# State-space scan with a gated feed-forward on one Trainium2 core: the loads and the first matmuls of the head are put in another order, and a token tile is transposed by one DMA

## The chip, the core and the metric

The kernel runs on one core of one Trainium2 chip. The metric is device time in microseconds (us), from launch to end, on that core. A core has five engines, each with its own instruction list that it works off in order: PE (TensorE, matmuls), DVE (VectorE), ACT (ScalarE), POOL (GpSimd) and SP (SyncE, which here only issues DMAs). ACT can issue DMAs too, from the same list as its arithmetic. Matmuls write PSUM banks; DVE and ACT read these out ("evacuate" them) into SBUF.

## The reference

Token count 2048, width D = 448, hidden width F = 1792, all inputs and the output bf16.

```python
x  = A_x
xn = layernorm(x)                               # over the 448 columns
# A: a diagonal complex scan over the 2048 tokens
Lam_bar = exp(exp(log_dt) * Lam)
Bu      = xn @ B_bar.T                          # B_bar = ((Lam_bar - 1) / Lam) * B
h[t]    = Lam_bar * h[t-1] + Bu[t]
s       = 2 * real(h @ C.T) + xn * Dskip
# B: a gated feed-forward
f = (sigmoid(xn @ w_gate) * (xn @ w_up)) @ w_down
out = x + s * silu(f)
```

## The kernel before

**Tiling.** The tokens are 16 tiles of 128 (x tile t is `x_all[:, t, :]`), in four chunks of 512 tokens. For matmuls a chunk must stand transposed, with the 448 columns on partitions: `xnT[c % 3]`, seven slots of 128 partitions by 512 tokens. A slot holds two neighbouring blocks of 64 columns, one on partitions 0 to 63, one on 64 to 127. Slot s holds the blocks s and s + 1, so that every block stands once on the lower and once on the upper half. The weights `wG` (gate) and `wU` (up) hold the first 896 output columns on the lower 64 partitions and the other 896 on the upper 64. One step of the feed-forward (`gu_mm`, lines 699 to 712) makes 2 times 128 output columns: 14 matmuls with 64 rows each, in pairs, one of a pair on each half of the array, into a pair of PSUM banks (`gu[a]`, three pairs; two more single banks are `acc[0]` and `acc[1]`). There are seven gate steps g.0 to g.6 and seven up steps u.0 to u.6 a chunk. A gate step is read out by a Tanh on ACT (line 721), an up step by a multiply on DVE (line 724).

**Order.** The kernel adds each operation with an engine, an estimated cost, what it reads and what it writes to a `Plan`. The planner gives every operation a due time, and builds each engine's list by a simulated run with estimated DMA rates (`rate=`). Two orders are fixed by hand: PE works in the order in which operations are added, and while `pl.seq` is set (the head) DVE does too. DMAs of one queue keep their order as well.

**The head (lines 383 to 412 and 962 to 990).** Eleven matmuls on zeros warm PE. SP and ACT issue the loads: x tile 0 on SP, tile 1 and then tiles 2 and 3 in one DMA on ACT; `wG` in three blocks a half (steps 0 and 1, 2 and 3, 4 to 6), the lower half on SP, the upper on ACT; then everything else on SP: `wU`, x tiles 4 to 7, `wU`, and `dbc` (Dskip copied to all partitions). POOL loads three small vectors.
For each of the tiles 0 to 3: `stats(t)` on DVE (line 424 and 425), `chain(t, 1)` (a square root on ACT, line 450, a copy on POOL, a reciprocal on DVE, line 452), `norm(t)` on DVE (line 469), eight PE transposes into an `acc` bank (`pe_transpose`, lines 501 to 503), and a copy of the bank into `xnT[0]`: on ACT for tile 0 (line 506), on DVE for tiles 1 to 3 (line 509).
`columns` (lines 535 to 563) turns the three small vectors with five tiny matmuls (lines 540 and 542) into per-partition columns, from which POOL makes the scan's coefficients.

PE's list in the head before:

```
warm, T0, T1, columns, g.0 g.1 of tile 0, g.0 g.1 of tile 1, T2, T3,
g.2 of tiles 0 and 1, g.0 g.1 g.2 of tiles 2 and 3, g.3 of all four, g.4 ...
```

(T2 stands for the eight transposes of tile 2.) DVE's list: stats 0 and 1, norm 0 and 1, stats 2 and 3, the copy of T1, the readout of `columns`, norm 2 and 3, the copies of T2 and T3; then `pl.seq` ends.

**Later tiles.** Tiles 4 to 15 are normalised on ACT (line 474) into one of eight buffers `xn`, 512 wide; POOL copies the first 64 columns behind the 448 (line 477), so that the last slot finds block 0 beside block 6; two DMA transposes on SP (`dma_transpose`, lines 510 to 518) fill the even and the odd slots. `skip_row` (line 482, DVE) multiplies `xn` by `dbc`.

Of the kernel before, what the change touches and what calls it, by code (L numbers as in the profile page):

```python
# [18 lines left out]
D = 448  # L19
# [226 lines left out]
def kernel(  # L246
# [39 lines left out]
    NXN = 8  # L286
    xn = [sbt(f"xn{i}", [512]) for i in range(NXN)]
    xnT_raw = [sbt(f"xnT{i}", [7 * L]) for i in range(3)]
    xnT = [flat(t[:], 7, L) for t in xnT_raw]
    hF_raw = [sbt(f"hF{i}", [FT * L]) for i in range(2)]  # L290
# [69 lines left out]
    BLK = {"g": [(0, 2), (2, 4), (4, 7)], "u": [(0, 3), (3, 7)]}  # L360
# [25 lines left out]
    load_w("SP", "g", 0, 0, rate=90e3)  # L386
    load_w("SP", "g", 0, 1)
    load_x(1, 1, "ACT")
    load_x(2, 2, "ACT")
    load_w("ACT", "g", 1, 0, rate=90e3)  # L390
    load_w("SP", "g", 0, 2)
    load_w("ACT", "g", 1, 1)
    load_w("ACT", "g", 1, 2)
# [13 lines left out]
    for h in range(2):  # L407
        load_w("SP", "u", h, 0, rate=215e3)
    load_x(4, 4, rate=140e3)
    for h in range(2):  # L410
        load_w("SP", "u", h, 1, rate=260e3)
    load("SP", "dbc", P * D * 2, dbc[:], A_Dskip.unsqueeze(0).to_broadcast((P, D)))
# [9 lines left out]
    def stats(t):  # L422
        b = t % 3
        add("DVE", 0.6, lambda: V.bn_stats(out=bst[b][:], in_=x_all[:, t, :]), r=[("x", t)], w=[("bst", b)])  # L424
        add("DVE", 0.16, lambda: V.bn_aggr(out=mv[:, t, :], in_=bst[b][:]), r=[("bst", b)], w=[("mv", t)])
# [40 lines left out]
    def norm(t):  # L466
        b = t % NXN
        if t < TPC:
            add("DVE", 0.42, lambda: V.tensor_scalar(out=xn[b][:, 0:448], in0=x_all[:, t, :],
                                                     scalar1=meanf[:, t, :], scalar2=rsd[:, t, :],  # L470
                                                     op0=ALU.subtract, op1=ALU.mult),
                r=[("x", t), ("mf", t), ("rs", t)], w=[("xn", b)])
        else:
            add("ACT", 0.65, lambda: A.activation(xn[b][:, 0:448], x_all[:, t, :], ACT.Identity,
                                                 bias=nmr[:, t, :], scale=rsd[:, t, :]),
                r=[("x", t), ("rs", t), ("nm", t)], w=[("xn", b)])
            add("POOL", 0.2, lambda: G.tensor_copy(out=xn[b][:, 448:512], in_=xn[b][:, 0:64]),
                r=[("xn", b)], w=[("xnw", b)])
# [5 lines left out]

    acc_n = [0]
# [9 lines left out]
    def pe_transpose(t):  # L495
        b, a, js = t % NXN, next_acc(), slice(t * P, t * P + P)
        tp = flat(acc[a][:].bitcast(BF16)[:, 0:7 * P], 7, P)

        def f():
            for s in range(6):  # L500
                T.transpose(tp[:, s, :], xn[b][:, s * H:s * H + P], ident[:, :])  # L501
            T.transpose(tp[0:H, 6, :], xn[b][:, 384:448], ident[:, :])
            T.transpose(tp[H:P, 6, :], xn[b][:, 0:H], ident[:, :])
        add("PE", 0.46, f, r=[("xn", b), "ident"], w=[("acc", a)])
        if t == 0:
# [6 lines left out]
    def dma_transpose(t):  # L512
# [4 lines left out]
        tload([k + ("a",)], xnT[c % 3][:, 0:7:2, js], xn[b][:], P * 1024, r=[("xn", b), ("xnw", b)] + al)  # L517
        tload([k + ("b",)], xnT[c % 3][:, 1:6:2, js], xn[b][:, 64:448], P * 768, r=[("xn", b)] + al)
# [16 lines left out]
    def columns(a):  # L535
        vps = flat(gu[a][:, 0, 0:12], 4, 3)
# [6 lines left out]
        add("PE", 0.4, f, r=["ident"] + [("vrow", k) for k in range(3)], w=[("gu", a)])  # L543
        pv = sbt("pv", [3, 4], FP32)
        dt_b = C("dt", 4, BF16)
        add("DVE", 0.1, lambda: V.tensor_copy(out=pv[:].rearrange("p k i -> p i k"), in_=vps[:]), r=[("gu", a)], w=["pv"])
# [20 lines left out]
    def silu_table():  # L567
        add("ACT", 1.3, lambda: A.preload_act_table_set("silu_and_others"), r=[("sd", t) for t in range(4)], w=["silutab"])
# [128 lines left out]
    SW = 0.1  # L697

    def gu_mm(c, k, m, a, lo, hi, first):
        x = xnT[c % 3]  # L700
        ts = slice(lo * P, hi * P)
# [3 lines left out]
        def f():  # L705
            for s in range(7):
                T.matmul(gu[a][:, 0, ts], lhsT=w_[0:H, s, ms], rhs=x[0:H, s, ts], start=(s == 0), stop=(s == 6))  # L707
                T.matmul(gu[a][:, 1, ts], lhsT=w_[H:P, (s + 1) % 7, ms], rhs=x[H:P, s, ts],  # L708
# [3 lines left out]
                   r=xr(c, lo, hi) + [("w", k, 0, m), ("w", k, 1, m)], w=[("gu", a)], name=f"{k}{c}.{m}")  # L712
# [3 lines left out]
    def gu_evac(c, k, m, a):  # L716
# [3 lines left out]
        if k == "g":  # L720
            add("ACT", act(1024), lambda: A.activation(th, gu[a][:], ACT.Tanh, scale=0.5),  # L721
                r=[("gu", a)], w=[tk])
        else:
            add("DVE", dve1(1024), lambda: V.scalar_tensor_tensor(out=ho, in0=th, scalar=1.0, in1=gu[a][:],  # L724
                                                                 op0=ALU.add, op1=ALU.mult),
                r=[("gu", a), tk], w=[hk])
# [23 lines left out]
    def b_phase(c, mid=None):  # L750
# [5 lines left out]
        rs = [(slice(0, H), 6), (slice(H, P), 5)]  # L756
# [14 lines left out]
        def fulls(pt, first):  # L771
            for i in range(2):
                for kt in range(3):
                    if pt < 3:
                        T.matmul(gu[slots[pt]][:, i, :], lhsT=bT[:, kt, i, pt * P:pt * P + P], rhs=x[:, 2 * kt, :],  # L775
                                 start=(first and kt == 0), stop=(not first and kt == 2))
                    else:
                        T.matmul(acc[a3[i]][:, 0:256], lhsT=bT6[:, kt, :],  # L778
                                 rhs=x[:, 2 * kt, i * 256:i * 256 + 256], start=False, stop=(kt == 2))
# [184 lines left out]
    pl.seq = True  # L964
    stats(0)
    stats(1)
    for t in (0, 1):
        chain(t, 1)
        norm(t)
    stats(2)  # L970
    stats(3)
# [3 lines left out]
    columns(slots0[2])  # L975
    for t in (2, 3):
        chain(t, 1)
        norm(t)
    for j in range(2):
        for m in range(2):  # L980
            gu_mm(0, "g", m, slots0[m], j, j + 1, not (j or m))
    pe_transpose(2)
    pe_transpose(3)
    silu_table()
    pl.seq = False
    gu_mm(0, "g", 2, slots0[2], 0, 2, True)
    for m in range(3):
        gu_mm(0, "g", m, slots0[m], 2, 4, False)
        gu_evac(0, "g", m, slots0[m])
    b_load()  # L990
    def stats_for(c):
        for t in range(4 * c, 4 * c + 4):
            if c not in (3,):
                stats(t)
# [16 lines left out]
    for i in range(3, 13):  # L1011
# [83 lines left out]
```

## Time and profile before

| what | us |
|---|---|
| median of three runs | 185.86 (185.44, 185.86, 187.11) |
| span of the profiled execution | 183.7 |
| PE busy | 177.4 |
| DVE busy | 166.4 |
| ACT busy | 94.8 |
| POOL busy | 34.2 |

The span runs from the first to the last instruction of one profiled execution; the median of the runs is 2.2 us longer, for what lies around it. Times below are from the start of that span. The granted TensorE clock was 1.000 over the span.

### The profile page before, as it was taken

What the parts mean: (1) busy time and instruction counts of PE and PEld (TensorE: products, weight loads), DVE (VectorE), ACT (ScalarE), POOL (GpSimd) and SP (SyncE); (2) the same over time, 40 slices, a digit from 0 to 9 for tenths busy, and PEclk for the clock granted to TensorE, in tenths of its full rate; (3) what the DMA queues carried; (4) which work ended last, traced back from release to release, by engine and by line L of the source; (5) the groups of instructions that cost most, each with busy time, mean ns of one, the idle gap of its engine ahead of it and who ended that gap; (6) DMA issues with size and microseconds to landing.
All of it is one profiled execution on the core that took longest, in us unless ns stands there. A gap on an engine that the chain in (4) does not pass through costs nothing.

```text
span 183.7 us, 3601 instructions
## 1 busy us (share of the span) xinstructions
PE 177.4 (97%) x1402; PEld 90.4 (49%) x1402; DVE 166.4 (91%) x296; ACT 94.8 (52%) x152; POOL 34.2 (19%) x95
## 2 busy tenths in 40 slices
PE   7699999999999999999999999999999999999992
PEld 2585555465554444455554444444555444455551
DVE  3873899899999998999999999999999998999973
ACT  3689993958599978665310452367120445211100
POOL 7370465000048557700000000000000000000000
PEclk9999999999999999999999999999999999999999
DMA  5999994489801370243000000002000000001121
GB/s 137 255 225 223 155 166 90 90 256 266 231 0 26 74 82 21 50 82 71 0 2 0 29 0 0 4 0 75 0 4 0 25 25 5 25 0 52 57 73 50
DMA packets 30258, 13.44 MB, mean 73 GB/s; under 512 B 19744, under 2 KB 30240, under 8 KB 30240
## 3 DMA queue, kind: packets, MB, share of 16 engines
q1 hardware_dynamic: 28336, 12.05, 30.7%
q10 hardware_dynamic: 1808, 1.15, 2.5%
q8 instruction: 11, 0.18, 0.4%
q14 instruction: 7, 0.06, 0.1%
q0 software_dynamic: 96, 0.00, 0.0%
HBM read 6.77 MB, written 1.84 MB: 47 GB/s over the span
## 4 chain that ended last, share of the span: by engine, by line
PE 93%; DMA 3%; DVE 1%; issue 1%; POOL 1%; DVEq 0%; POOLq 0%
PE gu L707 45%; PE gu L903 14%; PE acc L932 11%; PE acc L903 9%; PE gu L775 8%; DMA hF<-in_A_Lambda_re_dram 3%; PE gu L708 2%; PE acc L778 2%; PE gu L761 2%; POOL hF L353 1%; PE acc L501 0%; DVE o_t L948 0%; PE acc L764 0%; DVE o_t L944 0%; DVE o_t L941 0%
## 5 line engine op out<-in xcount | busy, mean ns | idle before, releaser
L708 PE MATMUL gu<-xnT,wG 64*128 64x512 bf16 (+2 forms) x245 | 46.0, 333 | 0.0
L707 PE MATMUL gu<-xnT,wG 64*128 64x512 bf16 (+2 forms) x245 | 46.0, 333 | 0.0
L707 PE MATMUL gu<-xnT,wU 64*128 64x512 bf16 x196 | 45.8, 376 | 0.0
L708 PE MATMUL gu<-xnT,wU 64*128 64x512 bf16 x196 | 45.8, 376 | 0.0
L721 ACT ACTIVATE sig<-gu 128x1024 f32<-128x1024 f32 x21 | 21.3, 1021 | 22.0 <-PE gu L708 21.9
L903 PEld LDWEIGHTS <-hF 128*128 128x128 bf16 x224 | 21.9, 98 | 20.7 <-issue 0.2
L707 PEld LDWEIGHTS <-wG 64*128 64x128 bf16 x245 | 21.9, 94 | 18.7
L707 PEld LDWEIGHTS <-wU 64*128 64x128 bf16 x196 | 18.4, 94 | 22.1
L724 DVE SCALAR_TENSOR_TENSOR hF<-sig,gu 128x1024 bf16<-128x1024 f32 x21 | 25.5, 1216 | 2.9 <-PE gu L708 1.6
L903 PE MATMUL gu<-wd,hF 128*128 128x448 bf16 x140 | 27.9, 352 | 0.0
L842 DVE TENSOR_TENSOR_SCAN wv<-c_r,st,z 128x512 bf16<-128x512 f32 x18 | 22.9, 1276 | 0.0
L932 PE MATMUL acc<-cT,hT 128*128 128x448 bf16 (+1 forms) x112 | 22.6, 346 | 0.0
L708 PEld LDWEIGHTS <-wG 64*128 64x128 bf16 x245 | 21.8, 94 | 0.0
L909 ACT ACTIVATE g_t<-gu 128x448 bf16<-128x448 f32 x10 | 5.4, 541 | 29.2 <-DVE o_t L946 12.9
L708 PEld LDWEIGHTS <-wU 64*128 64x128 bf16 x196 | 18.4, 94 | 0.0
L789 ACT CAST bus<-gu 128x1024 bf16<-128x1024 f32 x12 | 11.9, 1011 | 12.4 <-PE gu L761 12.2
L903 PE MATMUL acc<-wd,hF 128*128 128x448 bf16 x84 | 16.9, 352 | 0.0
L775 PE MATMUL gu<-xnT,bT 128*128 128x512 bf16 x72 | 16.7, 379 | 0.0
L932 PEld LDWEIGHTS <-hT 128*128 128x128 bf16 x119 | 11.5, 98 | 10.1 <-issue 0.4
L424 DVE BATCH_NORM_STATS2 bst<-x_all 128x6 f32<-128x448 bf16 x12 | 7.0, 610 | 5.7 <-DMA x_all<-in_A_x_dram 5.7
L795 ACT CAST bus<-acc 64x256 bf16<-64x256 f32 (+1 forms) x24 | 8.8, 369 | 6.4 <-PE acc L778 6.1
L944 DVE TENSOR_TENSOR o_t<-acc,xd 128x448 bf16<-128x448 f32 (+1 forms) x16 | 9.6, 601 | 1.3 <-PE acc L932 1.2
(138 smaller groups left out, 240.1 us busy)
## 6 DMA issues: line engine op xcount, KB each, us to landing
out_dram<-o_t SPq DMA_DIRECT2D x15, 112.0 KB, 1.7
wd<-in_B_w_down_dram SPq DMA_DIRECT2D x2, 784.0 KB, 5.5
x_all<-in_A_x_dram SPq DMA_DIRECT2D x3, 448.0 KB, 4.5
wU<-in_B_w_up_dram SPq DMA_DIRECT2D x2, 448.0 KB, 12.2
wU<-in_B_w_up_dram SPq DMA_DIRECT2D x2, 336.0 KB, 7.6
wG<-in_B_w_gate_dram SPq DMA_DIRECT2D x2, 224.0 KB, 6.5
wG<-in_B_w_gate_dram ACTq DMA_DIRECT2D x2, 224.0 KB, 6.6
xnT<-xn SPq DMA_TRANSPOSE x24, 2.4
```

Source lines behind the costliest of these rows:

```text
L424: add("DVE", 0.6, lambda: V.bn_stats(out=bst[b][:], in_=x_all[:, t, :]), r=[("x", t)], w=[("bst", b)])
L707: T.matmul(gu[a][:, 0, ts], lhsT=w_[0:H, s, ms], rhs=x[0:H, s, ts], start=(s == 0), stop=(s == 6))
L708: T.matmul(gu[a][:, 1, ts], lhsT=w_[H:P, (s + 1) % 7, ms], rhs=x[H:P, s, ts], start=(s == 0), stop=(s == 6))
L721: add("ACT", act(1024), lambda: A.activation(th, gu[a][:], ACT.Tanh, scale=0.5), r=[("gu", a)], w=[tk])
L724: add("DVE", dve1(1024), lambda: V.scalar_tensor_tensor(out=ho, in0=th, scalar=1.0, in1=gu[a][:], op0=ALU.add, op1=ALU.mult), r=[("gu", a) ...
L775: T.matmul(gu[slots[pt]][:, i, :], lhsT=bT[:, kt, i, pt * P:pt * P + P], rhs=x[:, 2 * kt, :], start=(first and kt == 0), stop=(not first a ...
L789: add("ACT", act(1024), lambda: A.copy(out=bus[u][:], in_=gu[slots[pt]][:]), r=key(pt), w=[("bus", u)])
L795: add("ACT", 0.3, lambda ns=ns, d=d, q=q, l=l, i=i: A.copy(out=bus[u][d, l, ns], in_=acc[a3[i]][q, 0:256]), r=[("acc", a3[i])] + ([("bus", ...
L842: dve(1.194, lambda k=k: V.tensor_tensor_scan(out=wv[:, k, :], data0=rb, data1=z[:, k, :], initial=(st[pt][:, k, :] if c else 0.0), op0=AL ...
L903: T.matmul(d, lhsT=hF[c % 2][:, m, h, js], rhs=wd[:, ft, :], start=(ft == 0), stop=(ft == FT - 1))
L932: T.matmul(y, lhsT=hT[c % 2][:, hm, js], rhs=cT[:, cm, c0:c1], start=(i == 0 and not on_pe), stop=(i == 6))
L944: add("DVE", dve1(n), lambda od=od, y=y, c0=c0, c1=c1: V.tensor_tensor(out=od, in0=y, in1=xq[:, c0:c1], op=ALU.add), r=[key, ("xd", q)], w ...
```

## The change

The head's loads are halved between SP and ACT, each DMA on SP with one of the same size on ACT behind it: x 0 | x 1, `wG` of steps 0 to 2 (lower | upper half), x 2 | x 3, `wG` of steps 3 to 6, then, with a wait for a square root of the head, x 4 and 5 | x 6 and 7, `wU` of steps 0 to 2, `wU` of steps 3 to 6, and `dbc` on SP. `wG` thus comes in two blocks a half instead of three.

On PE the first three gate steps are taken tile by tile. `columns` goes behind the first three and writes an `acc` bank instead of a `gu` pair. The copy of T2 goes from DVE to ACT; the load of ACT's second function table waits for it. g.3 writes the two `acc` banks and is read out by two Tanhs. On DVE the statistics of tile 4 stand in the fixed order ahead of the copy of T3; those of tiles 5 to 7 wait for that copy.

```
PE:  warm, T0, T1, g.0 g.1 g.2 of tile 0, columns, T2, g.0 g.1 g.2 of tile 1, T3,
     g.0 g.1 g.2 of tile 2, g.0 g.1 g.2 of tile 3, g.3 of all four, g.4 ...
DVE: stats 0 1, norm 0 1, stats 2, copy of T1, norm 2, stats 3, readout of columns,
     norm 3, stats 4, copy of T3
```

The slots of `xnT` are renumbered (`SL`): slot k holds the columns 128 k to 128 k + 127 of the row written twice. So `xn` is 896 wide, POOL copies all 448 columns, and one DMA transpose fills all seven slots. There are four buffers `xn` instead of eight.

```diff
-    NXN = 8
-    xn = [sbt(f"xn{i}", [512]) for i in range(NXN)]
+    NXN = 4
+    xn = [sbt(f"xn{i}", [2 * D]) for i in range(NXN)]
+    SL = [4 * s % 7 for s in range(7)]
...
-    BLK = {"g": [(0, 2), (2, 4), (4, 7)], "u": [(0, 3), (3, 7)]}
+    BLK = {"g": [(0, 3), (3, 7)], "u": [(0, 3), (3, 7)]}
...
     load_x(0, 1, "SP")
-    load_w("SP", "g", 0, 0, rate=90e3)
-    load_w("SP", "g", 0, 1)
     load_x(1, 1, "ACT")
-    load_x(2, 2, "ACT")
-    load_w("ACT", "g", 1, 0, rate=90e3)
-    load_w("SP", "g", 0, 2)
-    load_w("ACT", "g", 1, 1)
-    load_w("ACT", "g", 1, 2)
+    load_w("SP", "g", 0, 0, rate=150e3)
+    load_w("ACT", "g", 1, 0, rate=150e3)
+    load_x(2, 1, "SP", rate=180e3)
+    load_x(3, 1, "ACT", rate=180e3)
+    load_w("SP", "g", 0, 1, rate=165e3)
+    load_w("ACT", "g", 1, 1, rate=165e3)
...
-    for h in range(2):
-        load_w("SP", "u", h, 0, rate=215e3)
-    load_x(4, 4, rate=140e3)
-    for h in range(2):
-        load_w("SP", "u", h, 1, rate=260e3)
-    load("SP", "dbc", P * D * 2, dbc[:], A_Dskip.unsqueeze(0).to_broadcast((P, D)))
...
     def stats(t):
-        add("DVE", 0.6, lambda: V.bn_stats(out=bst[b][:], in_=x_all[:, t, :]), r=[("x", t)], w=[("bst", b)])
+        add("DVE", 0.6, lambda: V.bn_stats(out=bst[b][:], in_=x_all[:, t, :]),
+            r=[("x", t)] + ([("xnT", 0, 3, "a")] if 4 < t < 8 else []), w=[("bst", b)])
...
-            add("POOL", 0.2, lambda: G.tensor_copy(out=xn[b][:, 448:512], in_=xn[b][:, 0:64]),
+            add("POOL", 0.5, lambda: G.tensor_copy(out=xn[b][:, D:2 * D], in_=xn[b][:, 0:D]),
...
     def pe_transpose(t):
-        b, a, js = t % NXN, next_acc(), slice(t * P, t * P + P)
+        b, a, js = t % NXN, t % 2, slice(t * P, t * P + P)
...
-        if t == 0:
+        if t in (0, 2):
             add("ACT", 0.85, lambda: A.copy(out=xnT[0][:, :, js], in_=tp[:, :, :]),
...
-        tload([k + ("a",)], xnT[c % 3][:, 0:7:2, js], xn[b][:], P * 1024, r=[("xn", b), ("xnw", b)] + al)
-        tload([k + ("b",)], xnT[c % 3][:, 1:6:2, js], xn[b][:, 64:448], P * 768, r=[("xn", b)] + al)
+        tload([k + ("a",), k + ("b",)], xnT[c % 3][:, :, js], xn[b][:], P * 1792, r=[("xn", b), ("xnw", b)] + al)
...
-        vps = flat(gu[a][:, 0, 0:12], 4, 3)
+        vps = flat(acc[a][:, 0:12], 4, 3)
...
     def silu_table():
-        add("ACT", 1.3, lambda: A.preload_act_table_set("silu_and_others"), r=[("sd", t) for t in range(4)], w=["silutab"])
+        add("ACT", 1.3, lambda: A.preload_act_table_set("silu_and_others"), r=[("sd", t) for t in range(4)] + [("xnT", 0, 2, "a")], w=["silutab"])
...
+        if a is None:
+            for i in range(2):
+                add("ACT", act(512), lambda i=i: A.activation(th[:, i, :], acc[i][:], ACT.Tanh, scale=0.5),
+                    r=[("acc", i)], w=[tk] if i == 0 else [(tk, 1)])
...
+    def head_norm(t):
+        chain(t, 1)
+        norm(t)
+
+    def head_steps(t, first):
+        for m in range(3):
+            gu_mm(0, "g", m, slots0[m], t, t + 1, first and not m)
+
     stats(0)
     stats(1)
-    for t in (0, 1):
-        chain(t, 1)
-        norm(t)
+    head_norm(0)
+    head_norm(1)
+    load_x(4, 2, "SP", rate=165e3, r=[("sd", 1)])
+    load_x(6, 2, "ACT", rate=165e3, r=[("sd", 1)])
     stats(2)
-    stats(3)
     slots0 = [next_gu() for _ in range(3)]
     pe_transpose(0)
     pe_transpose(1)
-    columns(slots0[2])
-    for t in (2, 3):
-        chain(t, 1)
-        norm(t)
-    for j in range(2):
-        for m in range(2):
-            gu_mm(0, "g", m, slots0[m], j, j + 1, not (j or m))
+    head_norm(2)
+    load_w("SP", "u", 0, 0, rate=165e3, r=[("sd", 2)])
+    load_w("ACT", "u", 1, 0, rate=165e3, r=[("sd", 2)])
+    stats(3)
+    head_steps(0, True)
+    columns(1)
     pe_transpose(2)
+    head_steps(1, True)
+    head_norm(3)
+    load_w("SP", "u", 0, 1, rate=165e3, r=[("sd", 3)])
+    load_w("ACT", "u", 1, 1, rate=165e3, r=[("sd", 3)])
+    load("SP", "dbc", P * D * 2, dbc[:], A_Dskip.unsqueeze(0).to_broadcast((P, D)))
+    stats(4)
     pe_transpose(3)
     silu_table()
     pl.seq = False
-    gu_mm(0, "g", 2, slots0[2], 0, 2, True)
+    head_steps(2, False)
     for m in range(3):
-        gu_mm(0, "g", m, slots0[m], 2, 4, False)
+        gu_mm(0, "g", m, slots0[m], 3, 4, False)
         gu_evac(0, "g", m, slots0[m])
+    gu_mm(0, "g", 3, None, 0, TPC, False)
+    gu_evac(0, "g", 3, None)
```

The matmuls of `b_phase` (lines 750 to 808) and of `gu_mm` read the renumbered slots; nothing else is changed in them.

## The prediction

> **What bounds the kernel now.** I read the waits of PE first, since PE is busy for 97% of the span.
>
> ```profile
> PE 177.4 (97%) x1402; PEld 90.4 (49%) x1402; DVE 166.4 (91%) x296; ACT 94.8 (52%) x152; POOL 34.2 (19%) x95
> ...
> engine line waited for: us in total, times, longest us
> PE gu L418 <- DVE hF L378: 1.2, 1, 1.2
> PE gu L540 <- DMA hF<-in_A_Lambda_re_dram: 1.0, 1, 1.0
> PE acc L501 <- DVE xn L469: 0.5, 1, 0.5
> ```
>
> These are all the waits of PE: the last ends at 7.63. From there to 178.6 PE never waits, so only the head can win or lose, and what it loses is lost one for one. Next, the timeline of the head and the start of g.3 (the first matmul with 512 columns).
>
> ```profile
> 4.89 0.40 DVE L469 TENSOR_SCALAR xn<-x_all,meanf,rsd 128x448 bf16<-128x448 bf16 x1
> 5.78 0.62 DVE L424 BATCH_NORM_STATS2 bst<-x_all 128x6 f32<-128x448 bf16 x1
> 6.07 0.91 ACT L506 COPY xnT<-acc 128x896 bf16<-128x896 bf16 x1 [1.01 <-PE acc L503]
> 6.53 0.59 DVE L424 BATCH_NORM_STATS2 bst<-x_all 128x6 f32<-128x448 bf16 x1
> 7.26 0.59 DVE L509 COPY xnT<-acc 128x896 bf16<-128x896 bf16 x1
> 7.63 0.21 PE L540 MATMUL gu<-ident,hF 3*128 3x3 bf16 x3 [0.99 <-DMA hF<-in_A_Lambda_re_dram]
> ...
> 13.87 0.38 PE L707 MATMUL gu<-xnT,wG 64*128 64x512 bf16 x1
> ```
>
> The statistics of a tile take 0.75 on DVE (5.78 to 6.53), a copy of a transposed tile 0.59. By 13.87 PE has done all that stands before g.3, in both kernels the same work. The start of g.3 is therefore the scale: later by so much, the kernel is longer by so much.
>
> Then the DMAs: the issues in narrow windows (KB, us from issue to landing), and the rates in stretches (last columns: clock, DMA share, GB/s).
>
> ```profile
> wG<-in_B_w_gate_dram SPq DMA_DIRECT2D x1, 336.0 KB, 8.5
> wG<-in_B_w_gate_dram ACTq DMA_DIRECT2D x1, 336.0 KB, 9.1
> x_all<-in_A_x_dram SPq DMA_DIRECT2D x1, 448.0 KB, 10.6
> ...
> 5.00:6.00 1.00, 0.66 (x9) 0.49 (x10) 0.89 (x4) 0.06 (x1) 0.00 (x0) 1.00 1.09 297
> 8.00:11.00 3.00, 3.00 (x76) 2.54 (x74) 1.82 (x7) 1.93 (x3) 2.32 (x9) 1.00 1.12 236
> 12.00:14.00 2.00, 2.00 (x40) 1.99 (x38) 2.00 (x6) 2.00 (x3) 1.11 (x3) 1.00 1.11 217
> 39.00:42.00 3.00, 3.00 (x33) 1.64 (x28) 3.00 (x4) 1.70 (x3) 0.00 (x0) 1.00 1.09 378
> ```
>
> The last blocks of wG, issued at 2.6 and 3.2, land at 11.1 and 12.3. From 5 to 11 both halves of wG are in flight, one on each queue: 236 GB/s, once 297. From 12 to 14 one half of wU on SP alone: 217. A DMA over all 128 partitions (w_down, at 39) reaches 378. So halves side by side are no new thing here, and win about a tenth.
>
> **Part by part. When the loads land.** The first wG block: x 0 and 1 and the block make 224 + 672 = 896 KB; before, 896 KB (x 0 to 3 and two blocks of 224) had landed at 7.1 and 7.6 (issues at 1.2 and 1.7, 5.9 each). So 7.4, as before. x 2 and 3 now stand behind it: 0.229 MB more at 236 GB/s, 1.0, so 8.3 (5.1 before, when they stood ahead of it). x 4 to 7: before them stand x 0 to 3 and all of wG, 2,016 KB, the same bytes that landed before at 11.1 and 12.3, mean 11.7; 448 KB more (0.459 MB) at 236 GB/s take 1.9: **13.7**. The ends are 11.1 + 0.459/0.297 = 12.6 and 12.3 + 0.459/0.217 = 14.4. I take 236, the rate with the form of the blocks that are loaded now (768 bytes and more a row).
>
> **What PE gains.** `columns` no longer holds PE at 6.6 to 7.6, and the first gate steps start with the block at 7.4 to 7.6 instead of 7.89: at most 0.3 here. In the ideal case, every load early, PE starts with the copy of T0 (6.98) and runs 12 tile steps of 14 matmuls (28 pairs took 1.57 from 7.89, so 0.39 a step, 4.7), `columns` 0.25 and T2 and T3 at 0.62: 13.2, which is 0.7 before 13.87. That is all that the change can win. Steps by tile cost nothing: a pair takes 0.056 at 128 columns and 0.216 at 512, the same a column within 4%.
>
> **What PE loses, 1: the copy of T1 behind stats 2.** DVE works in its fixed order. Stats 2 wait for x 2 (8.3) and end at 9.05; the copy of T1 ends at 9.7. `columns` wants the bank that T1 leaves, and PE is in order: its first block ended at 8.7, so it idles to 9.7, where before it idled to 7.63. Norm 2 follows (reciprocal and norm, 0.65 as from 5.20 to 5.86): 10.4. T2 to 11.05, three steps to 12.2. Stats 3 end at 11.1; square root, reciprocal and norm took 1.2 before (4.72 to 5.86 with the handover), so T3 goes from 12.3 to 12.95. Three steps of tile 2 to 14.1, of tile 3 to 15.3: g.3 is 1.4 late.
>
> **What PE loses, 2: the copy of T3 behind stats 4.** Stats 4 stand ahead of the copy of T3 and wait for x 4. From the landing: 0.75 + 0.59 + 0.05 handover + 1.17 for three steps = 2.6 to the start of g.3. With 13.7 that is 16.3, **2.4 late**; this one ends last, and replaces the 1.4. Its bounds by the landing: 12.6 gives 1.3 (so the other chain's 1.4 holds), 14.4 gives 3.1.
>
> **What the rest costs.** ACT takes the copy of T2 (0.91), two issues of wU (0.65 each) and one of x (0.4) in the head, and its table load (1.28, before at 7.69) goes behind that copy, to about 13. Its first table activation moves from 10.04 to some 13.1, 3.1 late; the cover is the 2.4 by which PE is late too, and this idle time at the end of a stretch in which ACT is full:
>
> ```profile
> 32.01 1.40 ACT L795 CAST bus<-acc 128x256 bf16<-128x256 f32 x4 [3.19 <-PE acc L778]
> ...
> 169.00 0.68 DVE L859 TENSOR_TENSOR hT<-ta,tb 128x1024 bf16<-128x1024 bf16 x1
> ```
>
> Without that cover PE would wait for the bus casts, up to 0.7. g.3's two Tanhs of 512: no such row; between half of 1.02 and 0.65 each (the table rows with 513), at most 0.3 more of ACT under the same cover. DMA transposes: 8 issues of some 1.25 to 1.4 before chunk 1 (SP, 25.22 to 36.15) become 4; one with 128 by 896 has no row, nearest are bT's with more data, 1.25 to 1.63. The last landed at 37.3 for matmuls at 37.7; now some 33, under the first chunk's up steps. POOL's copy of 448 columns: 0.24 at 64 and 0.35 at 192 make some 0.6, four a chunk, in stretches in which POOL idles half the time. On DVE the copy of T2 leaves (0.6), and the last scan output (L859 above, done at 169.7) is wanted at 172.0, so DVE has 2.3 to spare. All this I cost at nothing; if the transposes lost their cover, each 1 late would be 1 on PE.
>
> Sum: 183.7 + 2.4 = 186.1 for the profiled execution. The median of the runs is 2.2 above the span, so **188.3**, range of this case alone 187.2 to 189.1.
>
> [...]
>
> **Rivals.** *1. The paired blocks load faster.* At 297 GB/s x 4 comes 2.0 sooner, at 11.7 (2.294 MB behind x 0 and 1 take 7.7 instead of 9.7), x 2 some 0.8 sooner (0.918 MB), and the first chain decides: 1.4 − 0.8 = 0.6 late, 186.5. For it: the row at 5 to 6, and that the queues were never in step before. Against it: three microseconds at 236 with both halves.
> *2. Faster: PE never idles behind its first block.* 0.7 early, 185.2. It needs x 2 by 6.4 (stats 0.75, copy 0.6 and norm 0.65 before PE is through with `columns` at 8.4) and x 4 by 10.6. At 378 GB/s x 2 would land at 6.9, so even this rate falls short; x would have to overtake weights.
> *3. Slower still: four xn buffers.* Norm 4 on ACT must wait for `skip_row` 0 on DVE, and this for dbc, which landed at 22.7 (issued at 11.2, 11.5 on its way) and remains the last load. Norm 4 ran at 22.4, after all seven Tanhs (last end 21.3). If the planner puts it ahead of g.4's, this Tanh ends at 22.7 + 0.4 + 0.8 + 1.0 = 24.9, and u.0, which wants that bank pair at 19.91 + 2.4 = 22.3, is 2.6 late; ahead of g.5's, 1.1. On top of the forecast some 1.9: 190.2. It decides only where norm 4 is listed before a Tanh; ACT was full from 10 to 28, and Tanhs are due earlier, which speaks against it.
>
> **How the numbers follow.** Forecast 0.58, rival 1 0.22, rival 2 0.08, rival 3 0.12. About 1% (1.86) is what a measurement can tell from no change. Within it lie rival 2, nearly all of rival 1 (0.20) and the lower end of the forecast (0.10): 0.38. Slower: 0.47 of the forecast, rival 3 and a rest of rival 1: 0.60. Faster by over 1% would take more than the 0.7 there is: 0.02. The range 185.2 to 189.5 takes in rivals 1 and 2 and the forecast's bounds, and leaves out rival 3 and a part of rival 2.
>
> **What would show it.** In the profile of the changed kernel: a wait of DVE's statistics for x tiles in the head, some 2.4 before stats 2 and over 1 before stats 4; PE waiting at `columns` for DVE's copy; g.3 starting near 16.3; both halves of wG at about 236 GB/s; no PE wait after g.3. Wrong, if x 4 lands before 12 (rival 1), if g.3 starts before 13.9 (rival 2), or if PE waits again between 20 and 27 (rival 3).

## The result, and the profile after

The changed kernel takes 193.36 us (median of four runs, 191.36 to 195.10), against 185.65 for the kernel before in the same session: 1.0353 times as long, 95% interval 1.0263 to 1.0444. (Here and below a ratio leaves disturbed runs out, so it can differ a little from that of the medians.) The forecast was 188.3 and its range ended at 189.5: the direction was right, the size a third of what came.

The profiled execution is the run of 191.36, span 189.6. The waits of PE (us in total, times, longest), and PE's busy time:

```profile
PE 179.3 (95%) x1451; PEld 96.6 (51%) x1458; DVE 167.6 (88%) x295; ACT 95.9 (51%) x154; POOL 40.3 (21%) x95
...
engine line waited for: us in total, times, longest us
PE gu L703 <- ACT xnT L503: 4.7, 2, 2.6
PE gu L412 <- DVE hF L379: 1.2, 1, 1.2
PE acc L497 <- DVE xn L464: 0.5, 1, 0.5
```

The wait for `columns` (1.0 before) is gone, as forecast. In its place PE waits 4.7 for the copies of T0 and T2, both on ACT, which the forecast had at nothing. The timeline shows where they lie. Each row has its start, its length, engine, line and operation:

```profile
8.40 0.63 DVE L418 BATCH_NORM_STATS2 bst<-x_all 128x6 f32<-128x448 bf16 x1 [2.67 <-DMA x_all<-in_A_x_dram]
8.69 0.26 PE L703 MATMUL gu<-xnT,wG 64*128 64x128 bf16 x1 [2.15 <-ACT xnT L503]
9.17 0.59 DVE L506 COPY xnT<-acc 128x896 bf16<-128x896 bf16 x1
...
14.00 0.62 DVE L418 BATCH_NORM_STATS2 bst<-x_all 128x6 f32<-128x448 bf16 x1
14.87 0.62 DVE L506 COPY xnT<-acc 128x896 bf16<-128x896 bf16 x1
...
19.72 0.38 PE L703 MATMUL acc<-xnT,wG 64*128 64x512 bf16 x1
```

g.3 starts at 19.72 instead of 13.87: 5.85 late, and the span is 5.9 longer. From g.3 to the end both kernels take 169.8. The scale that the prediction chose holds, and the whole loss of the profiled execution lies in the head. Stats 2 wait 2.67 for x 2, as forecast, and the copy of T1 stands behind them. Stats 4 at 14.00 wait for nothing: x 4 had landed at 12.94, and norm 3 (13.69) was later. What made norm 3 and the two copies late is in ACT's list. In this timeline of ACT, "ACTq" rows are DMA issues; the bracket gives the idle time ahead of an instruction and what ended it:

```profile
4.64 0.30 ACT L445 ACTIVATE sdb<-mv,epsc 128x1 bf16<-128x1 bf16 x1 [0.36 <-DVE rsd L447]
7.30 0.39 ACTq L354 DMA_DIRECT2D x_all<-in_A_x_dram  x1
7.73 0.91 ACT L503 COPY xnT<-acc 128x896 bf16<-128x896 bf16 x1 [2.79 <-DMA wG<-in_B_w_gate_dram]
9.28 0.30 ACT L445 ACTIVATE sdb<-mv,epsc 128x1 bf16<-128x1 bf16 x1 [0.65 <-DVE mv L420]
12.44 0.60 ACTq L354 DMA_DIRECT2D wU<-in_B_w_up_dram  x1
13.09 0.30 ACT L445 ACTIVATE sdb<-mv,epsc 128x1 bf16<-128x1 bf16 x1 [3.50 <-DMA wG<-in_B_w_gate_dram]
15.78 0.60 ACTq L354 DMA_DIRECT2D wU<-in_B_w_up_dram  x1
16.42 0.91 ACT L503 COPY xnT<-acc 128x896 bf16<-128x896 bf16 x1 [3.04 <-DMA wU<-in_B_w_up_dram]
17.34 1.28 ACT L564 ACT_TABLE_LOAD   x1
```

A copy of a transposed tile has no use for a weight load, yet three pieces of arithmetic are shown as waiting for one. What waits is the DMA issue ahead of each. The trace gives every DMA's semaphore, and the DMAs of SP and ACT share eight of them in both kernels (108, 109, 111 and 113 to 117):

| issue on ACT | at | semaphore, and the DMA that had it before | landed at | arithmetic that stood behind |
|---|---|---|---|---|
| x 6 and 7 | 7.30 | 113: first `wG` block, upper half | 7.28 | copy of T0, square root 2 |
| `wU` first block, upper | 12.44 | 115: second `wG` block, lower half | 12.41 | square root 3, so norm 3 and T3 |
| `wU` second block, upper | 15.78 | 109: `wU` first block, lower half | 15.76 | copy of T2, table load, all Tanhs |

Each issue starts 0.02 to 0.03 after the landing, and ACT's idle times of 2.8, 3.5 and 3.0 end with it. Where the earlier DMA had long landed, the issue goes at once: `wU` on SP at 8.21 took over semaphore 111, whose x 1 had landed at 3.26. The kernel before has the same waits, but for one of under 0.1 all of them on SP, whose list holds only DMAs. Its trace has the line that the prediction passed over (the queue's waits, same columns as PE's):

```profile
engine line waited for: us in total, times, longest us
...
SPq L353 <- DMA wG<-in_B_w_gate_dram: 4.5, 2, 3.7
```

What stands ahead of the prediction is wrong in one point: the loads do not wait for a square root. The `r=` of a load is an edge for the planner's order and makes no semaphore wait: x 4 and 5 were issued at 3.50, ahead of the square roots of tiles 0 and 1 (3.98 and 4.64).

The rates in stretches (last three columns: granted clock, DMA share, GB/s):

```profile
5.00:6.00 1.00, 1.00 (x14) 0.76 (x13) 0.63 (x3) 0.00 (x0) 0.00 (x0) 1.00 1.13 316
8.00:11.00 3.00, 2.31 (x42) 2.15 (x41) 2.42 (x7) 0.93 (x2) 0.18 (x1) 0.61 1.13 247
12.00:14.00 2.00, 1.63 (x46) 1.28 (x44) 0.48 (x3) 0.30 (x1) 1.66 (x5) 0.98 1.13 254
```

The loads ran at 247 to 316 GB/s, a little above the 236 that was taken, and landed about as forecast: the first `wG` block at 7.28 and 7.54 (7.4 forecast), x 2 at 8.38 (8.3), x 4 at 12.94 (13.7). The 0.61 is a clock halved from 8.68 to 12.10, straight behind PE's wait for T0's copy: the three steps of tile 0 took 2.2 where 1.17 was taken for them. The profiled run has one such stretch of 3.41 (clock 0.991 over the span). The other three runs, with clocks of 0.965 to 0.973, have two or three more of them, an estimate from the 0.009 of the clock that the one takes. That is enough for the 2 by which the median lies above the profiled run, but no trace of these runs shows where they fell.

### The profile page after: what moved, and what is told of

It is laid out like the page before. It is cut to its first block, busy times and chain, and to the rows that moved or that the text cites. A ratio compares the mean times of both kernels' runs of the same rounds, so it can differ in the third digit from the quotient of the medians.

```text
span 189.6 us, 3701 instructions
## 1 busy us (share of the span) xinstructions
PE 179.3 (95%) x1451; PEld 96.6 (51%) x1458; DVE 167.6 (88%) x295; ACT 95.9 (51%) x154; POOL 40.3 (21%) x95
## 4 chain that ended last, share of the span: by engine, by line
PE 78%; DMA 8%; DVE 7%; ACT 4%; issue 1%; ACTq 0%; SPq 0%; DVEq 0%
PE gu L703 33%; PE gu L903 14%; PE acc L932 11%; PE acc L903 8%; PE gu L775 8%; DMA wU<-in_B_w_up_dram 4%; DVE hF L724 4%; DMA wG<-in_B_w_gate_dram 3%; PE acc L778 2%; PE gu L761 2%; ACT hT L571 1%; ACT hF L721 1%; DVE xd L477 1%; ACT L564 1%; DVE hT L575 1%
## 5 line engine op out<-in xcount | busy, mean ns | idle before, releaser
L703 PEld LDWEIGHTS <-wG 64*128 64x128 bf16 x273 | 23.5, 97 | 18.4 <-DMA wG<-in_B_w_gate_dram 1.2
L704 PEld LDWEIGHTS <-wG 64*128 64x128 bf16 x273 | 23.3, 98 | 3.7 <-issue 3.7
L775 PE MATMUL gu<-xnT,bT 128*128 128x512 bf16 x65 | 15.3, 379 | 0.4
L472 POOL COPY xn<-xn 128x448 bf16<-128x448 bf16 x12 | 8.6, 735 | 25.9 <-ACT xn L469 25.7
```

The source lines that it names most:

```text
L472: add("POOL", 0.5, lambda: G.tensor_copy(out=xn[b][:, D:2 * D], in_=xn[b][:, 0:D]), r=[("xn", b)], w=[("xnw", b)])
L703: T.matmul(bank[0][:, ts], lhsT=w_[0:H, s, ms], rhs=x[0:H, SL[s], ts], start=(s == 0), stop=(s == 6))
L704: T.matmul(bank[1][:, ts], lhsT=w_[H:P, (s + 1) % 7, ms], rhs=x[H:P, SL[s], ts], start=(s == 0), stop=(s == 6))
```

## The experiments

The expectations name theories by letters: A, ACT's issues wait and hold its arithmetic; C, the halved clock; I, PE runs out of fetched instructions (the author's reading of a stop and of a 16 KB transfer; no trace names what PE lacks). Other letters are explained where they stand.

**e1: the kernel after, its three late ACT loads issued on SP instead.**

```diff
-    load_x(6, 2, "ACT", rate=165e3, r=[("sd", 1)])
+    load_x(6, 2, "SP", rate=165e3, r=[("sd", 1)])
...
-    load_w("ACT", "u", 1, 0, rate=165e3, r=[("sd", 2)])
+    load_w("SP", "u", 1, 0, rate=165e3, r=[("sd", 2)])
...
-    load_w("ACT", "u", 1, 1, rate=165e3, r=[("sd", 3)])
+    load_w("SP", "u", 1, 1, rate=165e3, r=[("sd", 3)])
```

> The changed kernel with its three later ACT loads (x 6 and 7, the two upper halves of wU) issued by SP instead, same waits, same sizes. Theory A (ACT stands still at these issues until an earlier load has landed, 2.8 + 3.5 + 3.0 us of ACT waits in the changed kernel's profile, and the copies of T0 and T2 and a square root stand behind them): ACT's waits for DMAs go, g.3 starts at about 15.6 (x 4 at 12.9 and 2.6 more) instead of 19.7, 187 to 188. Theory B (the forecast's own: the x tiles land late and DVE's fixed order passes that on): g.3 stays near 19 to 20, 192 to 194.

Median 189.79 (189.27 to 191.95), ratio 1.0241 (1.0164 to 1.0318). By the medians 3.6 of the 7.7 come back, by the ratios some 2; the two intervals overlap, and the profiled execution, the slowest of the four runs, has a span of 190.2, no shorter than the 189.6 of the kernel after. What the edit does is read from the head. No ACT instruction of the head waits for a DMA any more: the copy of T0 starts at 6.38 instead of 7.73, square root 3 at 11.54 instead of 13.09, the copy of T2 at 11.74 instead of 16.42. PE waits 1.2 at `columns` for the copy of T1, as loss 1 had it, and g.3 starts at 16.00, where the forecast's own chain has it at 16.3. But the time is above the forecast still, and the waits of PE show a new one:

```profile
PE acc L704 <- issue: 2.4, 1, 2.4
PE gu L412 <- DVE hF L379: 1.2, 1, 1.2
PE acc L536 <- DVE xnT L506: 1.2, 1, 1.2
PE gu L703 <- DMA wG<-in_B_w_gate_dram: 0.8, 1, 0.8
```

"issue" is time in which PE waited for nothing that the profile shows. In the timeline it lies in the middle of g.3, whose weights, tokens and banks were all there:

```profile
16.64 0.38 PE L703 MATMUL acc<-xnT,wG 64*128 64x512 bf16 x1
19.43 0.48 PE L704 MATMUL acc<-xnT,wG 64*128 64x512 bf16 x1 [2.40 <-issue]
```

From 19.59 to 23.01 the clock is halved. (Two other runs, with a clock of 1.000, have spans of 187.5 and 187.6.) So e1 names two more suspects, and most of the other runs are about these.

**e4: the kernel before, with the upper halves of wU on ACT.** The two are issued behind the square roots 2 and 3, and nothing else is changed.

```diff
-    for h in range(2):
-        load_w("SP", "u", h, 0, rate=215e3)
+    load_w("SP", "u", 0, 0, rate=215e3)
...
     for t in (2, 3):
         chain(t, 1)
         norm(t)
+        load_w("ACT", "u", 1, t - 2, rate=165e3, r=[("sd", t)])
```

> The kernel before with the two upper halves of wU issued by ACT behind the square roots of tiles 2 and 3, as in the change, and nothing else moved. Theory A: ACT waits at each issue for a wG block (landing at 9 to 12), the square root of tile 3 and the table load stand behind, T3 and all that follows is 2 to 4 late: 188 to 190. Theory B: no x tile is later, so 185 to 186.5.

Median 192.18 (188.87 to 192.99, without an interval). The first issue, at 7.33, hardly waits. The second waits till 17.16 for x 4 to 7, landed at 17.14, and the first Tanhs stand behind it. The profile puts this down to a load of x that no Tanh reads, in ACT's waits and in its timeline:

```profile
ACT hF L719 <- DMA x_all<-in_A_x_dram: 8.2, 1, 8.2
```

```profile
17.16 0.60 ACTq L353 DMA_DIRECT2D wU<-in_B_w_up_dram  x1
17.81 1.94 ACT L719 ACTIVATE hF<-gu 128x1024 bf16<-128x1024 f32 x2 [8.20 <-DMA x_all<-in_A_x_dram]
```

PE stops from 13.63 to 18.88 for the bank that the Tanh has not read out. So two DMA issues, 0.64 and 0.60 long, of which the second did it, cost the kernel before 6.7 by the medians, a half clock from 16.77 to 23.60 included. It is not the chain that was expected (square root 3 behind a `wG` block), but the same cause. Theory A is shown by putting its cause in as well as by taking it out.

**e2: the kernel after, with PE kept fed.** Eight matmuls on zeros behind the transposes of tile 1, and eight behind those of tile 3.

```diff
     pe_transpose(1)
+    warm_mm(8)
     head_norm(2)
...
     pe_transpose(3)
+    fill_mm(8)
     silu_table()
```

> The changed kernel with eight matmuls on zeros (512 columns) behind T1 and eight behind the copy of T3, so that PE idles less; no load and no wait is moved. Theory C (PE's idle time in the head costs its clock: granted 0.87 from 5 to 10 and 0.79 from 10 to 15 in the profile of the changed kernel, 0.965 to 0.991 over the runs): the granted clock is 0.995 or more in every run, the runs lie closer together, and the time falls by 1.5 to 2.5, to 191 to 192. Theory A without C: the same 193, since ACT's waits end when they did.

Median 194.60 (193.84 to 197.87), ratio 1.0464 (1.0400 to 1.0528). In the profiled execution the clock is 1.00 in all the head, but g.3 starts at 20.51, and ACT's three waits are there as before (2.7, 3.6, 3.1). As the cause of the late g.3 in the profile of after, the clock falls: while it was low PE would have had to wait for ACT in any case. For the other runs this settles little: two of the four runs of e2 lost clock too (0.991 and 0.983), and PE has 2.4 of new waits behind g.3.

**e3: the kernel before, with one DMA transpose a tile and four wide xn buffers.** The renumbered slots and POOL's wide copy belong to it; the head is that of before.

```diff
-    NXN = 8
-    xn = [sbt(f"xn{i}", [512]) for i in range(NXN)]
+    NXN = 4
+    xn = [sbt(f"xn{i}", [2 * D]) for i in range(NXN)]
...
-        tload([k + ("a",)], xnT[c % 3][:, 0:7:2, js], xn[b][:], P * 1024, r=[("xn", b), ("xnw", b)] + al)
-        tload([k + ("b",)], xnT[c % 3][:, 1:6:2, js], xn[b][:, 64:448], P * 768, r=[("xn", b)] + al)
+        tload([k + ("a",), k + ("b",)], xnT[c % 3][:, :, js], xn[b][:], P * 1792, r=[("xn", b), ("xnw", b)] + al)
```

> The kernel before with one part of the change alone: four xn buffers 896 wide, POOL copying 448 columns, one DMA transpose a tile, renumbered slots; the head as before. Theory A and B: no difference, 185 to 186.5, PE without a wait after 7.7. Rival (the ring of four xn buffers makes norm 4 wait for skip_row 0 and dbc): PE waits between 20 and 40, 187 to 188.5.

Median 185.89 in twelve runs, ratio 1.0011 (0.9979 to 1.0043): no difference beyond 0.4%. Rival 3 falls, and this part of the change is free.

**e5 to e9: the stop inside g.3.** e5 is the kernel before with its first twelve steps by tile, 56 matmuls more ahead of g.3 (the expectation says 28):

```diff
-    gu_mm(0, "g", 2, slots0[2], 0, 2, True)
+    for j in range(2):
+        gu_mm(0, "g", 2, slots0[2], j, j + 1, not j)
     for m in range(3):
-        gu_mm(0, "g", m, slots0[m], 2, 4, False)
+        gu_mm(0, "g", m, slots0[m], 2, 3, False)
+    for m in range(3):
+        gu_mm(0, "g", m, slots0[m], 3, 4, False)
```

> The kernel before with one part of the change alone: g.0 to g.2 in twelve steps of one tile (28 matmuls and 28 weight loads more before g.3), loads, lists of DVE and ACT as before. Theory I (PE runs out of fetched instructions: in the run with the ACT issues on SP, PE stood for 2.8 us inside g.3, after its 223rd matmul, waiting for nothing that the profile names, while a 16 KB transfer on the instruction queue started at 16.7): PE reaches its 223rd matmul at about 14.7 and stands there for 1 to 3 us; 187 to 188.5. Rival (steps by tile are free, and that stop was an accident of that run): no gap in PE after 7.7, 185 to 186.5.

Ratio 1.0077 (1.0012 to 1.0143), runs from 186.44 to 190.94; the profile has a gap in PE from 14.86 to 15.69 inside g.3, where before has none. e6 is e1 with the statistics of tile 4 behind the copy of T3:

```diff
-            r=[("x", t)] + ([("xnT", 0, 3, "a")] if 4 < t < 8 else []), w=[("bst", b)])
+            r=[("x", t)] + ([("xnT", 0, 3, "a")] if 4 <= t < 8 else []), w=[("bst", b)])
...
-    stats(4)
     pe_transpose(3)
```

> The run with the ACT issues on SP, and the statistics of tile 4 taken out of DVE's fixed order: they wait for the copy of T3 like those of tiles 5 to 7. Theory B (the forecast's second loss): g.3 starts near 15.2 instead of 16.0. Theory I: PE then reaches its 223rd matmul 0.8 sooner and stands longer for the same transfer, so the time stays at 189 to 190. Without I: 0.8 less, 188.5 to 189.

191.05, ratio 1.0257 (1.0161 to 1.0354). g.3 starts 0.9 sooner than in e1 (15.08), and nothing is won: PE stops sooner too, at 15.73. e7 is e6 with x 2 and 3 ahead of the first `wG` block:

```diff
-    load_w("SP", "g", 0, 0, rate=150e3)
-    load_w("ACT", "g", 1, 0, rate=150e3)
     load_x(2, 1, "SP", rate=180e3)
     load_x(3, 1, "ACT", rate=180e3)
+    load_w("SP", "g", 0, 0, rate=150e3)
+    load_w("ACT", "g", 1, 0, rate=150e3)
```

> As the run before, and x 2 and 3 loaded ahead of the first wG block. Theory B (the forecast's first loss): no wait of DVE for x 2, T1's copy by 7.8, the first wG block lands near 8.3; steps of tile 0 from 8.4, g.3 at about 13.9, as in the kernel before. Theory I: PE stands 2 to 3 us in g.3 for its instructions, 187 to 188.5. Without I: 185.5 to 186.2.

189.17, ratio 1.0171 (1.0097 to 1.0245): g.3 at 14.56, the stop at 15.21. e8 is e7 with the steps of tiles 2 and 3 taken together, 42 matmuls fewer:

```diff
-    head_steps(2, False)
     for m in range(3):
-        gu_mm(0, "g", m, slots0[m], 3, 4, False)
+        gu_mm(0, "g", m, slots0[m], 2, 4, False)
```

> As the run before, with the steps of tiles 2 and 3 taken together (256 columns, 42 matmuls fewer before g.3; 181 instead of 223 at its fourth pair). Theory I: the stop inside g.3 goes or shrinks below 1, 185.3 to 186.2. Rival: the same time as the run before, within 0.4.

187.03 in ten runs, ratio 1.0063 (1.0016 to 1.0109). g.3 starts 1.3 later than in e7, and the kernel is 2.1 faster, since the stop is gone. e9 has the same edit in e6:

> The kernel of the run without the late statistics of tile 4 (191.05 median, profile span 189.2, g.3 at 15.08, PE stopped from 15.73 to 18.40 inside g.3), with the steps of tiles 2 and 3 taken together at 256 columns: 42 matmuls fewer ahead of g.3. Theory I (PE uses up the instructions that it has fetched and waits for the next 16 KB): no stop inside g.3, the 2.4 us are won, and with them the half clock that followed the stop (3.41 us at half speed, 1.7): 186.5 to 187.5, g.3 not earlier than 15.0. Rival N (the stop belongs to something else in g.3, its two banks or its weights): the stop stays, 190 to 191.

189.52, ratio 1.0227 (1.0208 to 1.0247): a miss for both theories on the total, though the stop is gone here too. The first `wG` block landed at 8.43 in this execution (7.21 in e6), PE idled to 8.47, and the clock was halved from 10.82 to 14.23; g.3 came at 18.17.

**e10 and e13: fewer loads in flight.** The pages' DMA part has one more row that matters here, that of after as an example (queue, packets, MB, share of the 16 engines):

```profile
q8 instruction: 11, 0.18, 0.4%
```

Eleven transfers of 16,384 bytes, for 1,451 matmuls and 1,458 weight loads in the kernel after: 264 a transfer. That they are PE's instructions is the author's estimate from this count; the trace doesn't name their reader. In the quiet later part they start each 122 to 130 matmuls (at matmul 470, 596, 722 and so on in the profile of before). Counted back at this spacing, an estimate, the first would be due near matmul 95, and the second near 219. To see whether it queues behind the loads, the first try put all of `wU` and dbc behind the Tanh of g.1 by planner edges alone, in e6:

```diff
-    load_w("SP", "u", 0, 0, rate=165e3, r=[("sd", 2)])
-    load_w("SP", "u", 1, 0, rate=165e3, r=[("sd", 2)])
...
+    load_w("SP", "u", 0, 0, rate=165e3, r=[("hF", 1, 1)])
+    load_w("SP", "u", 1, 0, rate=165e3, r=[("hF", 1, 1)])
...
     gu_mm(0, "g", 3, None, 0, TPC, False)
```

> The same kernel as for the run without the late statistics of tile 4, all its matmuls kept, but all of wU and dbc issued on SP only behind the Tanh of g.1 (near 16 to 17). Theory I with the queue (the 16 KB wait behind the loads that are in flight on the same DMA engines): the first refill starts near 13.5, when x 6 and 7 have landed, instead of at 15.69; no stop inside g.3; 186.5 to 187.5. Rival F (the refill starts when PE asks for it, whatever the loads do): refill near 15.7 again, the stop of 2.3 stays, 190 to 191, or more if wU is then late for u.0 (wanted near 27, due by about 25).

It tested nothing of this: `wU` was issued from 8.03 (from 7.65 in e6), since such an edge makes no wait (194.48, ratio 1.0486; stop from 15.97 to 18.93). It also moved other work, and PE waited 1.8 near 37 for `bT`, which wasn't followed up. The second try makes the wait real: POOL first writes one column of each block of `wU` from that Tanh.

```diff
+    add("POOL", 0.3, lambda: [G.tensor_copy(out=wgt["u"][:, 0, m * P:m * P + 1], in_=hF[1][:, 1, 0, 0:1]) for m in (0, 3)],
+        r=[("hF", 1, 1)], w=[("w", "u", h, m) for h in range(2) for m in (0, 3)])
+    load_w("SP", "u", 0, 0, rate=165e3)
+    load_w("SP", "u", 1, 0, rate=165e3)
```

> The kernel without the late statistics of tile 4 (191.05, stop of PE inside g.3 15.73 to 18.40, refill at 15.69), with one column of each wU block first written by POOL from the Tanh of g.1, so that all of wU and dbc are issued on SP near 16.5. Theory I with the queue: refill starts by 13.9, no stop, 187 to 188.5. Rival F: refill near 15.7 and stop as before, 190.5 to 192. Either way u.0 (near 27) may be late for wU (landing near 25.5).

The refill starts at 12.54 instead of 15.69, and the stop is gone with all 216 matmuls ahead of g.3. The windows show the DMA engines empty where e1 has 197 to 228 GB/s:

```profile
13.00:15.00 2.00, 2.00 (x31) 1.62 (x28) 0.82 (x2) 1.99 (x4) 1.83 (x7) 0.50 0.01 5
15.00:17.00 2.00, 2.00 (x72) 2.00 (x70) 2.00 (x6) 0.91 (x3) 1.42 (x5) 0.94 0.00 0
17.00:19.00 2.00, 1.87 (x23) 0.76 (x19) 1.97 (x9) 2.00 (x3) 1.24 (x5) 1.00 0.04 8
```

The total hardly moves (189.74, ratio 1.0216, 1.0142 to 1.0290): this execution had half clock from 11.84 to 15.26, and `wU`, issued from 18.09, came late: PE waited 1.7 in all for it, for a readout and for `bT`.

**e11, e12 and e14: ACT's issues behind its head work, and PE fed again.** For e11, in the kernel after, x 6 and 7 go to SP, and the two `wU` issues stay on ACT behind the table load:

```diff
-    load_x(6, 2, "ACT", rate=165e3, r=[("sd", 1)])
+    load_x(6, 2, "SP", rate=165e3, r=[("sd", 1)])
...
     silu_table()
+    load_w("ACT", "u", 1, 0, rate=165e3, r=["silutab"])
+    load_w("ACT", "u", 1, 1, rate=165e3, r=["silutab"])
```

> The kernel after with x 6 and 7 issued on SP, and the two upper halves of wU still issued on ACT, but behind its head work (the copy of T2 and the load of the table). Theory A (what costs is ACT's arithmetic that stands behind an issue that waits): no wait of the copies or square roots of the head for a DMA; g.3 near 16, as in the run with no late issue on ACT (16.00); total near that run's 189.8, 189 to 191; the Tanhs of g.0 to g.2 now stand behind the issues and may be late by 1 to 3, which costs PE only where a bank is wanted. Rival B (an issue or a landing on ACT's queue is itself slower, wherever it stands): 193, as after.

191.58, ratio 1.0352 (1.0320 to 1.0384): a miss, and by the ratio no faster than the kernel after (1.0353). The waits of the head's arithmetic are gone, but the first block landed at 8.67, the clock was halved from 10.55 to 17.37, and g.3 came at 18.87. The next two add the eight zero matmuls behind the transposes of tile 1, first to e9 (e12), then to e11 (e14):

```diff
     pe_transpose(1)
+    warm_mm(8)
     head_norm(2)
```

> The kernel with pairs at the end (189.52 median, profile span 187.8, g.3 at 18.17, half clock from 10.82 to 14.23), with eight zero matmuls of 512 columns behind the transposes of tile 1, where PE was idle from 6.50 to 8.47. If the half clock is what was left (theory C for the rest): no half clock before 20 in most runs, 1.0 to 1.7 won at tile steps of 1.2 instead of 2.3: 187.5 to 188.5, g.3 at 16 to 17. If the start of g.3 is set by the landing of the second wG block (13.56) and by the copy of T3 alone: 189 to 190, as without.

187.44 in ten runs, ratio 1.0086 (1.0047 to 1.0125), clock 1.00 through the head, g.3 at 16.59: 2.1 won against e9, of which an earlier first block (7.88 instead of 8.43) has a part. In neither of the two does PE wait for ACT, and the halved clock has its price here. The windows from 10 to 15, first of e9, then of e12 (clock in the third column from the end):

```profile
10.00:15.00 5.00, 4.09 (x63) 3.46 (x62) 2.44 (x9) 3.19 (x5) 2.82 (x11) 0.66 1.12 224
```

```profile
10.00:15.00 5.00, 3.63 (x77) 2.94 (x78) 3.55 (x11) 3.44 (x6) 3.01 (x11) 1.00 1.12 235
```

> The kernel with ACT's wU issues behind its head work (191.58 median, g.3 at 18.87 with half clock from 10.55 to 17.37), with eight zero matmuls behind the transposes of tile 1. Theory A with the clock for the rest: clock 1.0 through the head, g.3 at 16.0 to 16.8, stop inside g.3 at most as in the first experiment: 188.5 to 190. Rival B (an issue on ACT costs wherever it stands): 191 to 193, g.3 not before 18.

192.08, ratio 1.0269 (1.0149 to 1.0388). These figures lie in the ranges that were named for rival B (191 to 193, g.3 not before 18), but the profile has nothing of its cause: no wait of PE for ACT is left. PE was through its tile steps but for one matmul by 14.85 at full clock; then it stopped, longer than in any other kernel:

```profile
PE gu L704 <- issue: 3.3, 1, 3.3
```

**What they show together.** All from the profiled executions, in us; the stop is that of PE for "issue", from the start of the last matmul ahead of it to the start of the next; the half clock is that behind the start of g.3. e2, e10 and e13 had other waits of PE later and are left out.

| kernel | g.3 at | span − g.3 | stop | refill starts | half clock behind |
|---|---|---|---|---|---|
| before | 13.87 | 169.8 | none | 14.99 | none |
| after | 19.72 | 169.8 | none | 17.74 | none |
| e1 | 16.00 | 174.2 | 16.64 to 19.43 | 16.66 | 3.41 |
| e3 | 13.40 | 169.9 | none | 13.82 | none |
| e4 | 18.88 | 172.3 | none | 14.72 | 4.72 |
| e5 | 14.21 | 170.7 | 14.86 to 15.69 | 12.88 | none |
| e6 | 15.08 | 174.1 | 15.73 to 18.40 | 15.69 | 3.41 |
| e7 | 14.56 | 172.5 | 15.21 to 17.60 | 14.95 | none |
| e8 | 15.84 | 169.4 | none | 15.77 | none |
| e9 | 18.17 | 169.7 | none | 16.88 | none |
| e12 | 16.59 | 169.7 | none | 16.64 | none |
| e11 | 18.87 | 170.9 | 19.52 to 20.29 | 17.50 | none |
| e14 | 18.39 | 172.0 | 14.85 to 18.39 | 15.57 | 3.41 |

Without a stop and without half clock the rest takes 169.4 to 169.9; a stop behind the start of g.3 adds its length, half clock half of its own, to within some 0.5. Every stop, that of e10 too, begins behind the same matmul, the 223rd of the program, and ends 2.65 to 2.81 after the refill starts (e1: 19.43 − 16.66). A short one in e2 (19.80 to 20.27, behind the same matmul) tells the transfer's start from its end: there the transfer itself took 2.5 instead of 1.3 to 1.4, and PE went on 3.9 after its start. Counted from the transfer's end all eight went on after 1.4 to 1.5. Before has only 160 matmuls ahead of g.3, so the next one behind its 223rd comes at 20.58, 5.6 after the refill; with steps by tile the 223rd is the seventh of g.3 (in e14, with eight zero matmuls ahead, the last but one of the tile steps). And the refill itself is late against that estimate: from matmul 95 to its start pass 3.1 to 5.1 in all kernels with loads in flight, and 0.96 in e13 (11.58 to 12.54).

The totals that the expectations named were mostly missed: in e1, e5 to e8 and e13 the median lies 0.7 to 1.8 above the range of the theory that the head bears out, in e4, e9 and e14 some 2. The theories are judged here by which wait came or went, and by where PE stopped, not by the totals.

## Why the prediction was wrong

*What held.* When the loads land (above). What PE gains: the wait at `columns` is gone. Loss 1: stats 2 at 8.40 and the copy of T1 at 9.17, forecast 8.3 and 9.1. Loss 2 was right in size where it could act: with ACT's late issues away g.3 came at 16.00, forecast 16.3; with stats 4 moved away too, at 15.08, where the forecast's other chain gives 15.3. In the kernel after itself it did not act, since T3 was late by another way. Of the rivals, 1 and 2 fall by the landings, and 3 by e3.

*The step that failed first is "What the rest costs".* It has "two issues of wU (0.65 each) and one of x (0.4) in the head" on ACT, and costs them at nothing because 3.2 of idle time would cover 3.1. It sized the issues by their duration. What the three cost here is when they could start: ACT idled for 2.8, 3.5 and 3.0 over them, until an earlier DMA had landed, and behind them stood the copies of T0 and T2 and square root 3, which PE waits for. The row that shows such waits, SP's 4.5, was in the trace of before. Taking the issues off ACT brought g.3 from 19.72 to 16.00, where the forecast had 16.3, so in the profiled execution this step accounts for the whole error in the head; the ratio went from 1.0353 to 1.0241, with intervals that overlap.

*The second is "Steps by tile cost nothing".* A pair at 128 columns takes as long a column as one at 512, that is so (0.056 and 0.216 a pair in the profile of before); but twelve steps by tile are 56 more matmuls, so that the 223rd lies in g.3, and behind it PE stood until 1.4 to 1.5 after the 16 KB transfer had ended. That it had used up its fetched instructions is theory I, not shown as such. In the profile of e1, where loss 2 is alone, this costs a stop of 2.4 and a half clock of 3.41 behind it, some 4.1 on top of the 2.1 by which g.3 is late: 169.8 + 16.00 + 2.4 + 1.7 = 189.9 for a span of 190.2. In the kernel after the refill decides nothing by itself: the next matmul behind the 223rd came at 20.44, and the refill of 17.74 had ended at 18.86, 1.58 before it, a little more than the 1.4 to 1.5 of the stops. But e14, whose PE was at that matmul as soon as any (14.85; e5 14.86) and stopped the longest, shows that in this head the stop takes back what a better order of ACT's work wins.

*The third is that the clock was taken as 1.000*, as in the profile of before. In the head of after PE is busy for 1.27 of the 3.41 from 5.27 to 8.68 (2.35 in before), and 3.41 at half clock follow in its profile, under the wait for ACT, with more in its other runs by their clocks (0.965 to 0.973); with the zero matmuls of e2 and e12 the clock was 1.00 from 5 to 20. e12 against e9 prices such a stretch in the open at 2.1 at most (1.6 between the two profiles, the earlier first block included).

One term of the sum was off besides: the 2.2 from span to median is 1.8 for launch and end, as in every run here, and 0.4 by which the profiled run of before was faster than the median.

The kernel before has no stop at its 223rd matmul, nor has the kernel after in its profile; eight kernels of this study stopped there, for 0.5 to 3.5.

*What stays open.* e11 and e14 have no wait of the head's arithmetic for a DMA, and their times (191.6, 192.1) are still nearer to after (193.4) than to e1 (189.8); e11 has after's ratio. So that issues on ACT cost nothing once they stand behind the head's arithmetic is not shown by the times. In the profiles e14 equals e1 (190.4 and 190.2); the medians' difference goes with the clock (0.982 to 0.997 in the runs of e14, 0.990 to 1.000 in those of e1), and why it fell more often there is not shown. Nor is it shown which idle times halve it: behind the stop of 2.4 in e1 it was halved, behind that of 2.0 in e7 it was not. No kernel here beat the one before.

## What to carry to other kernels

ACT idled for 2.8, 3.5 and 3.0 at three DMA issues of the kernel after, their own 0.39 to 0.60 included, and for 8.2 at one in e4: look which earlier DMA's semaphore an issue takes over, when that lands, and what stands behind it in the list; issued on SP, the same loads left no arithmetic of ACT's head waiting for a DMA (e1). Count matmuls as well as columns where loads are dense: 56 more of them ahead of g.3 went with a stop of 2.4 in e1 and of 0.5 in e5, and the transfer after which PE went on started 3.1 to 5.1 behind its estimated due time with loads in flight, 0.96 in e13 without. And where a part of a list is made late, look at the clock of what comes next: from 10 to 15 it was 0.79 in after and 0.66 in e9, and 1.00 in e2 and e12 with eight zero matmuls ahead.

## What was not expected of the hardware

The first 16 KB transfer of queue q8 (PE's instructions, by the estimate from their count) started 3.1 to 5.1 after the matmul near which it was estimated to be due, number 95, in the kernels with loads in flight, and 0.96 after it in e13, where no load was queued behind x 6 and 7. In the eight kernels in which PE stopped behind its 223rd matmul, it went on 1.4 to 1.5 after the transfer's end, though these kernels differ in what that matmul is (the last but one of the tile steps in e14, the seventh of g.3 in e1).

The half clock that lies in the head or behind the start of g.3 came in stretches of 3.41 or 3.42 (after, e1, e6, e9, e13, e14) or of twice that (6.83 in e4, 6.82 in e11). In the 3.41 ahead of the one in after PE was not idle throughout: it was busy for 1.27, and its one wait there was 2.15 long.

The first `wG` block was complete between 7.1 (e14) and 8.7 (e11) in kernels that issue the same loads up to then, and in the two latest (8.43 in e9, 8.67 in e11) the clock fell in the head, as it did in after and e13 with a block at 7.5: a profile of one execution carries that chance in every number of the head.
